# Attention and two MLP layers: float32 P V with columns of ones in the first batch, and MLP activations that read PSUM

## The chip, the cores and the metric

The kernel runs on one core of a Trainium2 chip. The metric is device time in microseconds of one execution, the median of several; lower is better. The engines are TensorE (PE; its weight loads are PEld), VectorE (DVE), ScalarE (ACT), GpSimd (POOL) and SyncE (SP, which issues DMAs).

## The reference, cut to what matters

```python
# q, k, v: (4, 8, 1152, 64) float32; weights float64
q_pool = q.reshape(B, H, S // 2, 2, D).mean(axis=3)           # 576 queries
scores = scale * np.matmul(q_pool, k.transpose(0, 1, 3, 2))
scores = scores - np.max(scores, axis=-1, keepdims=True)
attn = np.exp(scores)
attn = attn / (np.sum(attn, axis=-1, keepdims=True) + 1e-09)
x = np.matmul(attn, v)                    # then to (2304, 512) tokens
h = x @ moe_w_in;  g = np.maximum(0.01 * h, h);                     x = g @ moe_w_out
h = x @ moe2_w_in; g = np.where(h > 0, h, np.exp(np.minimum(h, 0)) - 1); out = g @ moe2_w_out
```

The weights w_in are 512 x 2048 and w_out 2048 x 512.

## The kernel before, in words

Matmuls take float32r operands, which TensorE reads with less precision than float32. Where precision matters an operand is kept as two float32r parts, a rounded one and the residual (`psplit`: a copy, then a subtraction).

**Order.** The kernel records operations with an engine, a cost in ns, a rank and the buffers that it reads and writes (`Program.add`). `Program.schedule` then plays them through as a list scheduler: an engine that falls idle takes the ready operation of lowest rank. Operations are emitted in the order of those start times, so ranks and costs decide what stands where on each engine, and each engine executes its own order strictly. Buffers of one tag are taken in turn; a tile waits for the tile that had its buffer before.

**Attention.** A pair (b, hp) is two heads of a batch; 16 pairs follow each other, 9 ranks apart. For a head, K and the pooled Q are transposed on TensorE (`tr_r`, L391). Row maxima come first: matmuls L466 of 384 keys into tag `s` (two banks), each reduced by VectorE (L470). Then, for each half of the queries (288 columns, `hf`) and each of 9 chunks of 128 keys (`c`), `weigh` makes scores minus the maximum in a bank `e` (L507, L508; in batch 0, `early`, the tags `e` and `h` in turn, four banks), ScalarE takes the exponential twice, once rounded into `pt[:, 0]` (L518) and once in float32 (L520), and VectorE makes the residual `pt[:, 1]` (L522) and adds the float32 values to `pacc` (L526, not for c = 0). `value` multiplies V by both parts (L538) into `o`, a single bank. V lies in `vn` as rounded part and residual side by side in the 128 output rows, so at the end of a half head the lower rows hold the residual's share: ScalarE copies them (L549, `tm`) and VectorE adds them (L551) into `xu`. `pt` has four buffers.

**Scaling.** Once per pair `normalise` sums `pacc` over the keys by float32 matmuls with ones (L568), inverts 10 numbers per partition (L572, L576), spreads and transposes them (L577, L584, L591) and multiplies `xu` (L587, L593).

**MLPs.** `PLAN` starts an MLP per batch and layer every 18 ranks: (0,0), (0,1), (1,0), (1,1) and so on, beside the attention of the following batches. For each of 16 blocks `f` of 128 hidden units and each half, 12 matmuls (L682) fill a bank `h`; there are two, and seven of several tags for batch 3. Layer 0 copies h to SBUF on ScalarE (L693), and VectorE takes max(0.01 t, t) in SBUF (L695). Layer 1 takes exp(h) on ScalarE (L699), min(t, 1) - 1 on VectorE in SBUF (L701) and max(h, t) (L704). The result is split (ScalarE L259, GpSimd L265), and `down` multiplies by w_out (L720) after every four blocks and adds up in SBUF (L733). In the MLPs of batch 0 each weight is first converted from float64 bits (`convert`: VectorE L291, L294, L303, ScalarE, GpSimd) and kept in DRAM for the other batches.

Of the kernel before, what the change touches and what calls it, by code (L numbers as in the profile page):

```python
# [13 lines left out]
ALU = mybir.AluOpType  # L14
# [140 lines left out]
def kernel(  # L155
# [85 lines left out]
    def sb(tag, shape, dt=F32, bufs=1):  # L241
        return prog.buf(tag, bufs, lambda: sp.tile(shape, dt, tag=tag, name=tag, bufs=bufs))
# [4 lines left out]
    def act(n, accum=False, sbuf=False):  # L247
        return 50 + 0.833 * n + (190 if accum else 0) + (43 if sbuf else 0)
# [202 lines left out]
    def prep_v(rank, b, hp, j):  # L451
        vr = raw[b, hp, j, "v"]
        vn = sb("vn", [128, KC, 2 * D], F32R, VB)
        o = D * j
        psplit(rank, KH, "POOL", lambda: vn[:, :, o:o + D], lambda: vn[:, :, D - o:2 * D - o],
               lambda: vr.ap, KC * D, (vn, "h"), [vr], fast=False)
        prep[b, hp, j, "v"] = vn

    def maxima(rank, terms, m, i, early):

# [38 lines left out]
    def weigh(rank, b, hp, j, hf, c, early):  # L499

        cols, parts = half(hf)
        kA, kB, qA, qB = (prep[b, hp, j, n] for n in ("kA", "kB", "qA", "qB"))
        st = pbank("e", F32, (128, 512), early=early)
        ks = slice(128 * c, 128 * c + 128)

        def mm():
            PE.matmul(out=st[:, 0:HB], lhsT=kA[:, ks], rhs=qA[:, cols], start=True, stop=False)  # L507
            PE.matmul(out=st[:, 0:HB], lhsT=kB[:, ks], rhs=qB[:, cols], start=False, stop=True)  # L508

        prog.add("PE", 2 * 133, rank - LS, mm, w=[st],  # L510
                 r=[kA, kB] + [(x, n) for x in (qA, qB) for n in parts])
        pt = sb("pt", [128, 2, HB], F32R, PTB)
        if c == 0 and hf == 0:
            pacc[b, hp, j] = sb("pacc", [128, NQ], F32, 3)
        acc = pacc[b, hp, j]

        p, pw = (lambda: acc[:, cols], (acc, hf)) if c == 0 else (lambda: st[:, 0:HB], st)
        prog.add("ACT", act(HB), rank - LE, lambda: A.activation(  # L518
            out=pt[:, 0], in_=st[:, 0:HB], func=ACTF.Exp), w=[(pt, 0)], r=[st])
        prog.add("ACT", act(HB), rank - LE, lambda: A.activation(  # L520
            out=p(), in_=st[:, 0:HB], func=ACTF.Exp), w=[pw], r=[st])
        prog.add("DVE", dve(HB), rank, lambda: V.tensor_tensor(  # L522
            out=pt[:, 1], in0=p(), in1=f32(pt[:, 0]), op=ALU.subtract), w=[(pt, 1)], r=[pw, (pt, 0)])
        prep[b, hp, j, "pt", hf, c] = pt
        if c:
            prog.add("DVE", dve(HB), rank, lambda: V.tensor_tensor(  # L526
                out=acc[:, cols], in0=p(), in1=acc[:, cols], op=ALU.add), w=[(acc, hf)], r=[pw, (acc, hf)])

    def value(rank, b, hp, j, hf, c, early):
# [4 lines left out]
        o = prep[b, hp, j, "o"]  # L534

        def mm():
            for a in range(2):
                PE.matmul(out=o[:, 0:HB], lhsT=vn[:, c, :], rhs=pt[:, a, :],  # L538
                          start=(c == 0 and a == 0), stop=(c == KC - 1 and a == 1))

        prog.add("PE", 2 * 133, rank, mm, w=[o], r=[vn, pt])
        if c < KC - 1:
            return
        if (b, hp) not in xu:
            xu[b, hp] = sb("xu", [128, NQ], F32, XFB)
        x = xu[b, hp]
        hi, lo = slice(64 * j, 64 * j + 64), slice(64 - 64 * j, 128 - 64 * j)
        tm = sb("tm", [128, HB])
        prog.add("ACT", act(HB), rank - LE, lambda: A.activation(  # L549
            out=tm[hi, :], in_=o[lo, 0:HB], func=ACTF.Copy), w=[tm], r=[o])  # L550
        prog.add("DVE", dve(HB), rank - LE, lambda: V.tensor_tensor(  # L551
# [49 lines left out]
    def attn_pair(at, b, hp):  # L601
# [39 lines left out]
        for u in range(36):  # L641
            j, hf, c = u // 18, u // 9 % 2, u % 9
            event(at + u / 4, weigh, at + u / 4, b, hp, j, hf, c, e)
            event(at + u / 4 + PVLAG, value, at + u / 4 + PVLAG, b, hp, j, hf, c, e)
        event(at + 9 + PVLAG + 0.1, normalise, at + 9 + PVLAG + 0.1, b, hp, e)


    def mlp(at, span, b, layer, xin, w_in, w_out, tags):
# [22 lines left out]
        def up(f):  # L671
# [4 lines left out]
            for hf in range(2):  # L676
# [14 lines left out]
                g32 = t  # L691
                if layer == 0:
                    prog.add("ACT", act(HB), rk, lambda h=h, t=t: A.activation(  # L693
                        out=t.ap, in_=h[:, 0:HB], func=ACTF.Copy), w=[t], r=[h])
                    prog.add("DVE", dve(HB), rk, lambda t=t, g32=g32: V.scalar_tensor_tensor(  # L695
                        out=g32.ap, in0=t.ap, scalar=0.01, in1=t.ap, op0=ALU.mult, op1=ALU.max),
                        w=[g32], r=[t])
                else:
                    prog.add("ACT", act(HB), rk, lambda h=h, t=t: A.activation(  # L699
                        out=t.ap, in_=h[:, 0:HB], func=ACTF.Exp), w=[t], r=[h])  # L700
                    prog.add("DVE", dve(HB, True), rk, lambda t=t: V.tensor_scalar(  # L701
                        out=t.ap, in0=t.ap, scalar1=1.0, scalar2=-1.0, op0=ALU.min, op1=ALU.add),
                        w=[t], r=[t])
                    prog.add("DVE", dve(HB), rk, lambda h=h, t=t, g32=g32: V.tensor_tensor(  # L704
                        out=g32.ap, in0=h[:, 0:HB], in1=t.ap, op=ALU.max), w=[g32], r=[h, t])
                psplit(rk, GH, GL, lambda f=f, cols=cols: g[f][:, 0, cols],
                       lambda f=f, cols=cols: g[f][:, 1, cols], lambda g32=g32: g32.ap, HB,
                       (g[f], hf), [g32], (g[f], 2 + hf))
# [106 lines left out]
```

## Time and profile before

| | |
|---|---|
| median of 3 runs | 1642.79 us (1641.87 to 1644.47) |
| profiled execution, its own time | 1636.31 us |
| its span, first to last instruction | 1634.5 us |
| mean granted TensorE clock | 0.961 of 2.4 GHz |
| busy: PE, PEld, DVE, ACT, POOL | 1485.2, 1380.4, 1271.7, 985.3, 835.5 us |
| instructions: PE, DVE, ACT, POOL | 9984, 2865, 2645, 844 |
| chain that ended last | PE 49%, DVE 32%, ACT 7%, issue 5% |

Busy time is the union of an engine's operations. TensorE's are pipelined, and a matmul's record (300 ns) is longer than the step to the next one, so its busy share says little of how much work it does; counts per stretch of time do. VectorE's records overlap a little as well.

### The profile page before, as it was taken

Reading aid. Unit: us, or ns where it says so; the run is one execution under the profiler, and the core shown is the slowest. Engines: PE = TensorE matmul, PEld = TensorE weight load, DVE = VectorE, ACT = ScalarE, POOL = GpSimd, SP = SyncE. Lnnn points to the kernel's source line nnn. Section 1 sums busy time; section 2 is a strip of 40 time slices with the busy share of each in tenths; the row PEclk is TensorE's granted clock in tenths of the full one; section 3 lists DMA queues with packets and bytes.
Section 4 is the critical chain, followed back from the end, with each engine's and each line's share of the span. In section 5 each row is a group of like instructions: output and inputs, shape, how many; then the busy total and the mean of one; then the engine's idle time right before and its main releaser. Section 6 shows DMA issues by size and latency. Waiting matters only on the chain.

```text
span 1634.5 us, 28876 instructions
## 1 busy us (share of the span) xinstructions
PE 1485.2 (91%) x9984; PEld 1380.4 (84%) x9984; DVE 1271.7 (78%) x2865; ACT 985.3 (60%) x2645; POOL 835.5 (51%) x844
## 2 busy tenths in 40 slices
PE   5898988889888789999999999999999998899898
PEld 3677767778777678899998999899999998898897
DVE  7999999999999999976778778877778666225333
ACT  5675766767567676576665665565666653443432
POOL 6321237656666665455555354545554444456562
PEclk9897988989989999999999999999999999999999
DMA  5221223444344343232222231222222111222221
GB/s 160 89 58 51 78 76 118 143 136 136 116 131 144 125 144 124 59 111 73 83 73 74 57 91 54 87 89 81 81 74 60 46 59 52 87 65 78 71 70 44
DMA packets 85202, 145.00 MB, mean 89 GB/s; under 512 B 9024, under 2 KB 27456, under 8 KB 85056
## 3 DMA queue, kind: packets, MB, share of 16 engines
q1 hardware_dynamic: 85056, 143.17, 29.3%
q8 instruction: 78, 1.28, 0.3%
q14 instruction: 68, 0.56, 0.1%
HBM read 112.20 MB, written 21.50 MB: 82 GB/s over the span
## 4 chain that ended last, share of the span: by engine, by line
PE 49%; DVE 32%; ACT 7%; issue 5%; DMA 3%; POOL 3%; SPq 0%; ACTq 0%; POOLq 0%; DVEq 0%
PE h L720 14%; PE h L682 11%; PE o L538 5%; DVE m L470 5%; DVE pt L522 4%; DVE pacc L526 4%; DVE t L701 3%; PE e L507 3%; DVE wr L303 3%; PE s L466 3%; DVE t L695 3%; PE e L508 2%; DVE ct L294 2%; PE t L568 2%; DVE ct L291 2%
## 5 line engine op out<-in xcount | busy, mean ns | idle before, releaser
L720 PE MATMUL h<-g,wo 128*128 128x288 f32 x2544 | 452.7, 300 | 14.9 <-DVE t L704 8.4
L682 PE MATMUL h<-xs,wi 128*128 128x288 f32 x2520 | 441.7, 310 | 26.9 <-DVE t L704 16.0
L682 PEld LDWEIGHTS h<-xs,wi 128*128 128x128 f32 x2520 | 380.5, 198 | 40.4 <-DVE t L704 22.6
L720 PEld LDWEIGHTS h<-g,wo 128*128 128x128 f32 x2544 | 382.6, 191 | 23.3 <-DVE t L704 7.3
L518 ACT ACTIVATE pt<-e 128x288 fp32r<-128x288 f32 x504 | 203.5, 411 | 204.0 <-PE e L508 193.6
L538 PE MATMUL o<-pt,vn 128*128 128x288 f32 x1152 | 274.2, 317 | 18.2 <-DVE pt L522 16.1
L265 POOL TENSOR_TENSOR wo<-wr,wo 128x512 fp32r<-128x512 f32 x128 | 169.6, 1327 | 229.1 <-ACT wo L259 223.8
L265 POOL TENSOR_TENSOR g<-t,g 128x288 fp32r<-128x288 f32 x256 | 218.7, 862 | 82.7 <-ACT g L259 78.6
L522 DVE TENSOR_TENSOR pt<-e,pt 128x288 fp32r<-128x288 f32 x448 | 201.2, 449 | 49.5 <-ACT e L520 47.6
L538 PEld LDWEIGHTS o<-pt,vn 128*128 128x128 f32 x1152 | 200.6, 199 | 33.0 <-DVE pt L522 28.0
L265 POOL TENSOR_TENSOR wi<-wr,wi 128x512 fp32r<-128x512 f32 x128 | 171.7, 1341 | 75.4 <-ACT wi L259 60.5
L470 DVE TENSOR_REDUCE m<-s 128x1 f32<-128x384 f32 x384 | 201.0, 547 | 5.6 <-PE s L466 5.1
L526 DVE TENSOR_TENSOR pacc<-e,pacc 128x288 f32<-128x288 f32 x448 | 199.7, 446 | 0.3
L520 ACT ACTIVATE e<-e 128x288 f32<-128x288 f32 x448 | 180.7, 409 | 0.3
L507 PE MATMUL e<-qA,kA 128*128 128x288 f32 x504 | 166.4, 331 | 15.2 <-DVE pacc L526 14.4
L466 PE MATMUL s<-kA,qA 128*128 128x384 f32 x384 | 147.9, 405 | 30.1 <-DVE m L470 24.2
L259 ACT ACTIVATE g<-t 128x288 fp32r<-128x288 f32 x256 | 112.3, 445 | 100.2 <-DVE t L704 50.4
L695 DVE SCALAR_TENSOR_TENSOR t<-t 128x288 f32<-128x288 f32 x128 | 101.2, 799 | 79.4 <-ACT t L693 79.1
L508 PE MATMUL e<-qB,kb 65*128 65x288 f32 x504 | 153.3, 305 | 0.0
L301 POOL TENSOR_TENSOR ct<-ct,cr 128x256 uint32<-128x256 uint32 x128 | 101.7, 797 | 99.8 <-DVE ct L294 47.0
L259 ACT ACTIVATE wo<-wr 128x512 fp32r<-128x512 f32 x128 | 80.4, 629 | 110.6 <-PE h L720 46.6
L701 DVE TENSOR_SCALAR t<-t 128x288 f32<-128x288 f32 x128 | 78.4, 613 | 74.5 <-ACT t L699 73.7
(124 smaller groups left out, 2446.9 us busy)
## 6 DMA issues: line engine op xcount, KB each, us to landing
wr<-w SPq DMA_DIRECT2D x192, 256.0 KB, 2.7
cr<-in_moe_w_in_dram SPq DMA_DIRECT2D x64, 256.0 KB, 2.9
cr<-in_moe_w_out_dram SPq DMA_DIRECT2D x64, 256.0 KB, 2.7
w<-wr SPq DMA_DIRECT2D x64, 256.0 KB, 2.4
raw<-in_k_dram SPq DMA_DIRECT2D x32, 288.0 KB, 2.9
raw<-in_v_dram SPq DMA_DIRECT2D x32, 288.0 KB, 2.9
kb<-kA SPq DMA_DIRECT2D x32, 288.0 KB, 3.2
raw<-in_q_dram SPq DMA_DIRECT2D x32, 256.0 KB, 3.0
```

The source lines that it names most:

```text
L259: prog.add("ACT", act(n, sbuf=not psum), rank, lambda: A.activation(out=hi(), in_=src(), func=ACTF.Copy), w=[w], r=r)
L265: lambda: eng.tensor_tensor(out=lo(), in0=src(), in1=f32(hi()), op=ALU.subtract),
L466: PE.matmul(out=st[:, 0:384], lhsT=qa(), rhs=kA[:, 384 * c:384 * c + 384], start=(n == 0), stop=(n == len(terms) - 1))
L470: prog.add("DVE", dve(384), rank, lambda st=st, c=c: V.tensor_reduce(out=m[:, i, c:c + 1], in_=st[:, 0:384], axis=AX.X, op=ALU.max), w=[(m ...
L507: PE.matmul(out=st[:, 0:HB], lhsT=kA[:, ks], rhs=qA[:, cols], start=True, stop=False)
L508: PE.matmul(out=st[:, 0:HB], lhsT=kB[:, ks], rhs=qB[:, cols], start=False, stop=True)
L518: prog.add("ACT", act(HB), rank - LE, lambda: A.activation(out=pt[:, 0], in_=st[:, 0:HB], func=ACTF.Exp), w=[(pt, 0)], r=[st])
L522: prog.add("DVE", dve(HB), rank, lambda: V.tensor_tensor(out=pt[:, 1], in0=p(), in1=f32(pt[:, 0]), op=ALU.subtract), w=[(pt, 1)], r=[pw, ( ...
L526: prog.add("DVE", dve(HB), rank, lambda: V.tensor_tensor(out=acc[:, cols], in0=p(), in1=acc[:, cols], op=ALU.add), w=[(acc, hf)], r=[pw, ( ...
L538: PE.matmul(out=o[:, 0:HB], lhsT=vn[:, c, :], rhs=pt[:, a, :], start=(c == 0 and a == 0), stop=(c == KC - 1 and a == 1))
L682: PE.matmul(out=h[:, 0:HB], lhsT=wi[:, a, c, :], rhs=xs[c][:, e, cols], start=(c == 0 and a == 0 and e == 0), stop=(c == DC - 1 and a == 1))
L720: PE.matmul(out=y[:, 0:HB], lhsT=w[f][1][:, a, d * 128:(d + 1) * 128], rhs=g[f][:, e, cols], start=(f % FC == 0 and a == 0 and e == 0), st ...
```

## The change

In batch 0 (`FULL`): P stays float32 and has one part, one exponential, no residual and no `pacc`. V stays float32; the other 64 columns of `vn` are ones, so that the product holds the sums of P in the other 64 rows. P V is one float32 matmul per chunk. At the end of a half head ScalarE copies the sums plus 1e-9, VectorE inverts them (64 x 288) and multiplies. `normalise` is not called. In all batches the activations change: layer 0 is max(h, 0.01 h) with h from PSUM, layer 1 is Relu(1 - exp(h)) on ScalarE, then max(-t, h) on VectorE.

```diff
+    FULL = (0,)
...
+        if b in FULL:
+            prog.add("POOL", pool(KC * D), rank, lambda: G.tensor_copy(
+                out=f32(vn[:, :, o:o + D]), in_=vr.ap), w=[(vn, "h")], r=[vr])
+            prog.add("POOL", pool(KC * D / 2), rank, lambda: G.memset(
+                f32(vn[:, :, D - o:2 * D - o]), 1.0), w=[(vn, "l")])
+            return
...
+        if b in FULL:
+            prog.add("ACT", act(HB), rank - LE, lambda: A.activation(
+                out=f32(pt[:, 0]), in_=st[:, 0:HB], func=ACTF.Exp), w=[pt], r=[st])
+            return
...
+            if b in FULL:
+                PE.matmul(out=o[:, 0:HB], lhsT=f32(vn[:, c, :]), rhs=f32(pt[:, 0]),
+                          start=(c == 0), stop=(c == KC - 1))
+                return
...
-        prog.add("PE", 2 * 133, rank, mm, w=[o], r=[vn, pt])
+        prog.add("PE", (4 if b in FULL else 2) * 133, rank, mm, w=[o], r=[vn, pt])
...
+        if b in FULL:
+            prog.add("ACT", act(HB), rank - LE, lambda: A.activation(
+                out=tm[hi, :], in_=o[lo, 0:HB], func=ACTF.Copy, bias=1e-9), w=[tm], r=[o])
+            prog.add("DVE", dve(HB), rank - LE, lambda: V.reciprocal(
+                out=tm[hi, :], in_=tm[hi, :]), w=[tm], r=[tm])
+            prog.add("DVE", dve(HB), rank - LE, lambda: V.tensor_tensor(
+                out=x[hi, cols], in0=o[hi, 0:HB], in1=tm[hi, :], op=ALU.mult), w=[(x, (j, hf))], r=[o, tm])
+            return
...
-        event(at + 9 + PVLAG + 0.1, normalise, at + 9 + PVLAG + 0.1, b, hp, e)
+        if b not in FULL:
+            event(at + 9 + PVLAG + 0.1, normalise, at + 9 + PVLAG + 0.1, b, hp, e)
...
-                        out=t.ap, in_=h[:, 0:HB], func=ACTF.Copy), w=[t], r=[h])
-                    prog.add("DVE", dve(HB), rk, lambda t=t, g32=g32: V.scalar_tensor_tensor(
-                        out=g32.ap, in0=t.ap, scalar=0.01, in1=t.ap, op0=ALU.mult, op1=ALU.max),
-                        w=[g32], r=[t])
+                        out=t.ap, in_=h[:, 0:HB], func=ACTF.Copy, scale=0.01), w=[t], r=[h])
+                    prog.add("DVE", dve(HB), rk, lambda h=h, t=t, g32=g32: V.tensor_tensor(
+                        out=g32.ap, in0=h[:, 0:HB], in1=t.ap, op=ALU.max), w=[g32], r=[h, t])
...
-                    prog.add("DVE", dve(HB, True), rk, lambda t=t: V.tensor_scalar(
-                        out=t.ap, in0=t.ap, scalar1=1.0, scalar2=-1.0, op0=ALU.min, op1=ALU.add),
-                        w=[t], r=[t])
-                    prog.add("DVE", dve(HB), rk, lambda h=h, t=t, g32=g32: V.tensor_tensor(
-                        out=g32.ap, in0=h[:, 0:HB], in1=t.ap, op=ALU.max), w=[g32], r=[h, t])
+                    prog.add("ACT", act(HB, sbuf=True), rk, lambda t=t: A.activation(
+                        out=t.ap, in_=t.ap, func=ACTF.Relu, bias=1.0, scale=-1.0), w=[t], r=[t])
+                    prog.add("DVE", dve(HB), rk, lambda h=h, t=t, g32=g32: V.scalar_tensor_tensor(
+                        out=g32.ap, in0=t.ap, scalar=-1.0, in1=h[:, 0:HB], op0=ALU.mult, op1=ALU.max),
+                        w=[g32], r=[h, t])
```

The scheduler makes a new order of all this. Lines of the changed kernel are shifted: L515 and L516 are the score matmuls, L550 the float32 P V, L474 and L478 the maxima and their reductions, L392 the transposes, L568 the reciprocal, L570 the product, L535 and L538 the residual and sum of the other batches, L723, L726 and L728 the three steps of layer 1's activation.

TensorE at the boundary of the third and fourth half head of batch 0, before (`o`, `h`, `e`, `s` are tiles in PSUM; a new number of `o` is a new half head):

```order
L538 MATMUL o_759<-pt_842,vn_238 128x288 x2
L507 MATMUL h_896<-qA_347,kA_277 128x288
L508 MATMUL h_896<-qB_502,kb1_81 128x288
L507 MATMUL h_901<-qA_347,kA_277 128x288
L508 MATMUL h_901<-qB_502,kb1_81 128x288
L466 MATMUL s_910<-kA_751,qA_824 128x384
L466 MATMUL s_918<-kA_751,qA_824 128x384
L466 MATMUL s_924<-kA_751,qA_824 128x384
L466 MATMUL s_927<-kA_751,qA_824 128x384
L538 MATMUL o_930<-pt_857,vn_238 128x288 x2
```

and with the change:

```order
L550 MATMUL o_705<-pt_752,vn_209 128x288
L515 MATMUL h_797<-qA_336,kA_267 128x288
L516 MATMUL h_797<-qB_478,kb1_81 128x288
L515 MATMUL h_804<-qA_336,kA_267 128x288
L516 MATMUL h_804<-qB_478,kb1_81 128x288
L392 MATMUL t_808<-identr_63,qh_577 128x128 x4
L515 MATMUL e_816<-qA_336,kA_267 128x288
L516 MATMUL e_816<-qB_478,kb1_81 128x288
L515 MATMUL e_824<-qA_336,kA_267 128x288
L516 MATMUL e_824<-qB_478,kb1_81 128x288
L515 MATMUL h_830<-qA_336,kA_267 128x288
L516 MATMUL h_830<-qB_478,kb1_81 128x288
```

One transpose and the next half head's first P V follow. Five score pairs and five transposes now stand between the last P V of a half head and the first of the next, where two pairs and four matmuls of maxima stood.

VectorE at the end of the first half head of batch 0, with the change (`m` are maxima; before, this place had one L551 between residuals, sums and reductions):

```order
L568 RECIPROCAL tm_415<-tm_415 64x288
L478 TENSOR_REDUCE m_410<-s_428 128x1
L478 TENSOR_REDUCE m_410<-s_433 128x1
L570 TENSOR_TENSOR xu_442<-o_293,tm_415 64x288
L478 TENSOR_REDUCE m_410<-s_440 128x1
```

At the 16 ends of batch 0 the reciprocal and the product have none to two operations between them, one on average.

VectorE where layer 1 of batch 0 begins, before (`t` is the activation's tile in SBUF, `ct` and `wr` belong to the weight conversion):

```order
L701 TENSOR_SCALAR t_6235<-t_6235 128x288
L294 SCALAR_TENSOR_TENSOR ct<-cr,ct 128x256
L704 TENSOR_TENSOR t_6235<-h,t_6235 128x288
L303 SCALAR_TENSOR_TENSOR wr<-cm,ct 128x256
L526 TENSOR_TENSOR pacc<-e,pacc 128x288
L701 TENSOR_SCALAR t_6266<-t_6266 128x288
```

and with the change:

```order
L728 SCALAR_TENSOR_TENSOR t_5575<-t_5575,h 128x288
L304 SCALAR_TENSOR_TENSOR wr<-cm,ct 128x256
L535 TENSOR_TENSOR pt<-e,pt 128x288
L304 SCALAR_TENSOR_TENSOR wr<-cm,ct 128x256
L538 TENSOR_TENSOR pacc<-e,pacc 128x288
L728 SCALAR_TENSOR_TENSOR t_5605<-t_5605,h 128x288
```

One operation of VectorE per activation is left where two stood.

## Rows read from the trace of the kernel before

**Rows 1.** The page, part 2: busy tenths in 40 slices of 40.9 us.

```profile
PE   5898988889888789999999999999999998899898
...
DVE  7999999999999999976778778877778666225333
```

**Rows 2.** Windows: length; busy us (xcount) of PE, PEld, DVE, ACT, POOL; clock; DMA.

```profile
0.00:28.00 28.00, 11.26 (x35) 6.99 (x36) 18.93 (x37) 11.30 (x22) 19.64 (x30) 1.00 0.50 154
28.00:240.00 212.00, 188.87 (x990) 150.14 (x989) 200.74 (x511) 149.67 (x437) 56.55 (x59) 0.90 0.26 73
240.00:680.00 440.00, 380.23 (x2401) 345.61 (x2402) 426.80 (x959) 294.58 (x808) 278.67 (x293) 0.93 0.41 128
680.00:1385.00 705.00, 677.47 (x4922) 658.24 (x4921) 540.10 (x1198) 437.93 (x1165) 348.93 (x335) 0.99 0.25 73
1385.00:1640.00 255.00, 227.41 (x1641) 219.43 (x1639) 85.11 (x163) 91.83 (x213) 131.73 (x127) 0.99 0.23 68
```

**Rows 3.** Timeline: the first exponential; the last scaling of batch 0.

```profile
28.03 0.41 ACT L518 ACTIVATE pt<-e 128x288 fp32r<-128x288 f32 x1
...
240.02 0.22 DVE L593 TENSOR_TENSOR xu<-t,xu 128x64 f32<-128x64 f32 x1
```

**Rows 4.** Timeline of VectorE near 65 us: start, length, line.

```profile
60.58 1.01 DVE L470 TENSOR_REDUCE m<-s 128x1 f32<-128x384 f32 x2
...
64.90 0.44 DVE L522 TENSOR_TENSOR pt<-e,pt 128x288 fp32r<-128x288 f32 x1
65.26 0.44 DVE L526 TENSOR_TENSOR pacc<-e,pacc 128x288 f32<-128x288 f32 x1
```

**Rows 5.** Windows: 50 us in which TensorE is full.

```profile
800.00:850.00 50.00, 49.74 (x372) 48.90 (x372) 39.08 (x82) 31.54 (x86) 29.61 (x29) 1.00 0.28 83
```

**Rows 6.** Timeline of TensorE: float32 and float32r operations in bursts.

```profile
89.12 2.29 PE L568 MATMUL t<-ones,pacc 128*128 128x2 f32 x20
...
92.99 0.63 PE L584 MATMUL t<-ident,rb 128*128 128x128 f32 x4
...
207.82 0.42 PE L391 MATMUL t<-identr,ql 128*65 128x128 f32 x4 [0.80 <-DVE ql L474]
```

**Rows 7.** Groups by line and shape: xcount, busy us, mean ns, idle before.

```profile
L549 ACT ACTIVATE tm<-o 64x288 f32<-64x288 f32 x64 | 26.0, 406 | 8.6 <-PE o L538 7.1
...
L474 DVE TENSOR_REDUCE ql<-m 128x4 fp32r<-128x12 f32 x32 | 5.0, 155 | 0.0
...
L576 DVE RECIPROCAL r<-r 128x10 f32<-128x10 f32 x16 | 3.4, 210 | 0.2
```

**Rows 8.** Timeline: end of a half head, ScalarE to VectorE.

```profile
234.02 0.40 ACT L549 ACTIVATE tm<-o 64x288 f32<-64x288 f32 x1
...
234.62 0.46 DVE L551 TENSOR_TENSOR xu<-o,tm 64x288 f32<-64x288 f32 x1
```

**Rows 9.** Waits of TensorE, 0 to 250 us: total us, times, longest.

```profile
PE t L391 <- ACT kA L406: 3.2, 8, 0.6
```

**Rows 10.** Groups of VectorE, 240 to 680 us.

```profile
L695 DVE SCALAR_TENSOR_TENSOR t<-t 128x288 f32<-128x288 f32 x32 | 21.6, 677 | 0.4 <-ACT t L693 0.3
...
L701 DVE TENSOR_SCALAR t<-t 128x288 f32<-128x288 f32 x32 | 18.5, 579 | 1.2 <-ACT t L699 1.0
```

**Rows 11.** One line's operations: duration ns min/median/max.

```profile
L701 DVE TENSOR_SCALAR t<-t x128: 290/449/1550, 479.2 to 1615.6; 128x288 f32<-128x288 f32 x128
...
L704 DVE TENSOR_TENSOR t<-h,t x105: 440/448/460, 479.8 to 1609.0; 128x288 f32<-128x288 f32 x105
```

**Rows 12.** Group by line: ScalarE, SBUF to SBUF, 288 wide.

```profile
L259 ACT ACTIVATE g<-t 128x288 fp32r<-128x288 f32 x256 | 112.3, 445 | 100.2 <-DVE t L704 50.4 <-DVE t L695 47.2 <-PE h L720 0.6
```

**Rows 13.** Waits of TensorE, 690 to 860 us (first MLP layer, batch 1).

```profile
PE h L720 <- ACT t L693: 0.3, 1, 0.3
```

**Rows 14.** Waits of TensorE, 877 to 1040 us (second layer, batch 1).

```profile
PE h L682 <- DVE t L704: 5.9, 9, 1.6
PE h L720 <- DVE t L704: 2.9, 1, 2.9
```

More of the change, by code (lines that the diff above doesn't have):

```diff
@@ L454, in prep_v @@
         o = D * j
+        prep[b, hp, j, "v"] = vn
+        if b in FULL:
[4 more added lines that the diff above has]
+            return
         psplit(rank, KH, "POOL", lambda: vn[:, :, o:o + D], lambda: vn[:, :, D - o:2 * D - o],
                lambda: vr.ap, KC * D, (vn, "h"), [vr], fast=False)
-        prep[b, hp, j, "v"] = vn
     def maxima(rank, terms, m, i, early):
@@ L512, in weigh @@
         pt = sb("pt", [128, 2, HB], F32R, PTB)
+        prep[b, hp, j, "pt", hf, c] = pt
+        if b in FULL:
+            prog.add("ACT", act(HB), rank - LE, lambda: A.activation(
+                out=f32(pt[:, 0]), in_=st[:, 0:HB], func=ACTF.Exp), w=[pt], r=[st])
+            return
         if c == 0 and hf == 0:
@@ L523, in weigh @@
             out=pt[:, 1], in0=p(), in1=f32(pt[:, 0]), op=ALU.subtract), w=[(pt, 1)], r=[pw, (pt, 0)])
-        prep[b, hp, j, "pt", hf, c] = pt
         if c:
```

## The prediction

> **What bounds the kernel now.** I read the page's slices first, then the windows by stage, and only then groups and waits inside a stage. The slices [rows 1] show two regimes: VectorE (DVE) is at nine tenths or more up to slice 17, about 700 us, and TensorE (PE) from there to the end. The windows cut this into stages [rows 2]; their borders are the first exponential at 28 us and the last scaling of batch 0 at 240 us [rows 3]. Stage A, 28 to 240 us, is the attention of batch 0 alone: VectorE is busy for 200.7 of 212 us, ScalarE for 149.7, GpSimd for 56.6, and TensorE shows 188.9 us, but with 990 matmuls only. Stage B, 240 to 680 us, holds batch 1's attention, batch 0's two MLPs and the weight conversions: VectorE 426.8 of 440 us. In a full stretch TensorE starts 372 matmuls in 50 us, one each 0.134 us [rows 5], so the 2401 of stage B are about 322 us of work: TensorE waits there. Stage C, 680 us to 1385 us, has 4922 matmuls, 660 us of work in 705: TensorE is the bound. The last stage is the MLPs of batch 3 alone, with TensorE ahead of all others. So work taken from VectorE pays in A and B, one for one at most until TensorE's own work stands in the way, and in C and after only through waits on a PSUM bank.
>
> **Stage A, step by step.** VectorE issues equal operations of 288 elements 0.36 us apart, although one lasts 0.44 us [rows 4]; the step is what it costs. Each of the 16 half heads of batch 0 (4 pairs, 2 heads, 2 halves) has 9 residuals L522 and 8 sums L526. They go: 17 x 0.36 = 6.1 us of the 200.7 / 16 = 12.5 us that VectorE spends on a half head. The scaling chain of a pair goes too. A reciprocal of 288 elements comes.
>
> *The reciprocal.* The trace has only one of 10 elements, 210 ns, beside a reduction of 12 elements in 155 ns [rows 7]. I take 143 ns as fixed (155 less 12 elements at about 1 ns), which leaves 6.7 ns an element: 0.14 + 288 x 6.7 ns = 2.07 us. Low end: the 55 ns above the reduction are paid once, and it costs as the 288-wide sum L551, 0.46 us [rows 8], plus 0.055: 0.51 us. High end: the 0.08 us by which duration exceeds step in rows 4 is no part of its fixed cost, which leaves 0.063, 14.7 ns an element and 4.3 us. I take 2.07, because rows 7 compare two operations of nearly equal size. The Trainium skill, VectorE: DVE Perf Modes, section First, the fixed hardware budget, says that the reciprocal runs on an iterated divide with a repeat count of 8. Eight cycles of its 0.96 GHz would be, as an estimate from that page, 2.5 us, and the sum below would be about 7 us longer; no run here shows that size.
>
> *The float32 matmul.* The program issues 160 matmuls L568, the trace has 320, and 20 take 2.29 us, 0.11 us apart [rows 6]: one float32 matmul is two operations. Four float32 transposes take 0.63 us and four float32r ones 0.42 [rows 6], 0.21 us more for 512 columns, 0.41 ns a column. So I price one of the two at 0.134 + 288 x 0.41 ns = 0.252 us and a chunk of P V at 0.50 us, where two float32r matmuls cost 0.27. Low end: as float32r, 0.27. High end: three further such columns and a weight load (0.11) that nothing hides, 2 x (0.134 + 0.354 + 0.11) = 1.20 us.
>
> *TensorE's own time* for a half head is then 18 score matmuls x 0.134 = 2.4, 9 chunks x 0.50 = 4.5, 7.5 matmuls for the maxima (384 wide, 0.174 by width from 0.134) = 1.3, 9 transposes x 0.06 (from the four in rows 6) = 0.5: 8.8 us, 140 us for 16. VectorE needs 12.5 - 6.1 + 2.0 = 8.4 us less its share of the scaling chain: no longer the bound, but close.
>
> *The single o bank.* The next half's P V waits until the sums are copied, inverted and multiplied. That was copy 0.41 [rows 7] and add 0.46 with a hop of 0.20 between them [rows 8], under a TensorE that waited anyway. Now it is hop 0.2, copy 0.41, hop 0.2, reciprocal 2.07, one reduction 0.47 (none to two stand between in the order above; step from rows 4), product 0.46, hop 0.2: 4.0 us. Against it TensorE has the rows between two o tiles in the order: five score pairs and five transposes in the place shown, 1.6 us, and 2.1 us as a mean over 15 boundaries by the same prices. 1.9 us stay open, 15 times: 28 us. Behind the waiting matmul stands everything of TensorE, since it takes its work in order.
>
> *Sum.* 28 us of start, 140 of work, 28 open, and 3 us that transposes still wait for ScalarE [rows 9]: 199, call it 200 instead of 240. **Stage A gives 40 us.** Off the path, at nothing: 144 second exponentials of ScalarE (it has 62 us to spare [rows 2] and gets 59 more), and V's copy and fill on GpSimd instead of copy and subtraction (busy for 57 of 212 us; without that cover it would be at most 8 x 1.5 us).
>
> **Stage B.** Each of the 32 operations L701 in it goes. They last 579 ns on average [rows 10], less 0.08 of overlap: 32 x 0.50 = 16 us. L695 (677 ns) becomes an operation with h in PSUM. The same kind, L704, lasts 440 to 460 ns, whereas L701, which reads SBUF alone, runs from 290 to 1550 [rows 11]; at 448 it gives 32 x 0.23 = 7.4 us. The second new operation has the form of a product and maximum, which no row shows from PSUM; I take L704's 448, and 677 as the high end, which takes those 7 us back. VectorE falls from 427 to 403 us, still above TensorE's 322, so it stays the bound and **stage B gives 23.5 us**.
>
> **Stage C and the last one.** In layer 1 the bank h was held for exponential, L701 and L704; now Relu on ScalarE stands in the middle, 445 ns by the copy of that size [rows 12] against a median of 449 for L701 [rows 11]: nothing. In layer 0 the bank was free after ScalarE's copy, and TensorE hardly waited, 0.3 us [rows 13]; now it is held over a VectorE operation as well. In the second layer such waits make 8.8 us per MLP [rows 14]. VectorE has a quarter of its time free in C [rows 2], so I take 0 for the sum of both and keep 8.8 a layer for the rival. The last stage has seven banks for it.
>
> **Total.** 1636.3 us of the profiled execution less 40 and 23.5 is 1572.8. The median of the runs shown, 1642.8, is 6.5 us above that execution, and I add them: **1579 us**, 3.9% faster.
>
> **Rivals.** *The reciprocal is cheap* (0.51 us): the open time falls to 0.33 us x 15 = 5, 23 us less, 1556 us. For it: two operations 55 ns apart say little of 288 elements. Against: nothing else in rows 7 explains the 55 ns. *Layer 0 pays for the bank*: 8.8 us in each of the two layer-0 MLPs of stage C, and Relu costs 445 where an undisturbed L701 took 290 [rows 11], 0.155 x 64 in the two second layers: 17.6 + 9.9 = 27.5 more, 1606 us. For it: with two banks TensorE returns to one after 12 matmuls, 1.6 us, which a copy, a maximum and their hops nearly fill. Against: attention matmuls lie between. The Trainium skill, ScalarE: Activation LUTs, section Rules for kernel authors, speaks for this rival: it wants relu and max on VectorE and not on ScalarE. By that rule Relu loses; the trace agrees for the undisturbed operation alone, since with GpSimd beside it VectorE's median is ScalarE's time. *Float32 P V is dear*: at 1.20 us a chunk, 0.70 x 144 = 101 us more on TensorE's path in A, 1680 us, slower by 2.2%. It decides from 0.50 + 64 / 144 = 0.94 us a chunk, where all 64 us are eaten. For it: no row shows a wide float32 matmul; against: the transposes, which stream the same type at 0.41 ns a column more.
>
> **How the numbers follow.** Forecast 0.60, alone good for 1560 to 1596 (the waits of 28 us by half either way, and the 7 us of the product form); cheap reciprocal 0.13; layer 0 pays 0.20; dear float32 0.04; the rest, 0.03, is a new order that helps or hurts in a way I do not see. The range 1540 to 1612 takes in the first three with their own spread, and a reciprocal up to its high end. Measurements of this kernel tell 0.2% from no change. All but the dear float32 case and half of the rest are faster by more: faster 0.94, same 0.02, slower 0.04.
>
> **What would show it.** The reciprocal near 2 us with 288 elements; P V records in pairs 0.25 us apart; batch 0 over by 200 us; TensorE's longest waits in A on o for the product; the two activations' VectorE operations at 0.45 us whatever GpSimd does; MLP layers of batch 0 still at nine tenths of VectorE. If A ends by 180 us, the open time was overrated; if it ends after 230, float32 is dear or the chain is longer; if C, from its first MLP to its last, is more than 10 us longer, layer 0 pays.

## The result, and the profile after

The changed kernel takes 1593.53 us against 1642.33 us: a ratio of 0.9698 with the interval [0.9657, 0.9738], 3.0% faster. In a second session it took 1590.76 us. The forecast was 1579 us, 12 to 15 us too low; both times lie inside its range. The profiled execution of the first session was a disturbed one (3913 us, each MLP matmul 553 ns long instead of 300; with it the median would be 1595.37 us), so the profile after is that of the second session, where the execution took 1588.61 us.

The page of the changed kernel: span, busy time of each engine, busy tenths of TensorE and VectorE in 40 slices of 39.7 us.

```profile
span 1586.8 us, 28364 instructions
...
PE 1457.8 (92%) x9884; PEld 1369.4 (86%) x9884; DVE 1100.4 (69%) x2461; ACT 974.8 (61%) x2621; POOL 812.3 (51%) x852
...
PE   5888889888888889999999999999999999899998
...
DVE  6776579999999999876768676766767564124122
```

VectorE lost 171 us of busy time and the kernel 48 us. In [rows 1] VectorE stood at nine tenths from the second slice on; now it does so only from the seventh to the sixteenth. In the first 230 us neither it nor TensorE is full: batch 0 has lost its bound, and TensorE has not taken its place as the forecast had it.

To put times to it I cut both traces where the first matmul of an MLP starts: (batch 0, layer 0), (1, 0) and (3, 0). Stage A runs from the first exponential to the first of these. The windows of the changed kernel (columns as in [rows 2]), and then those of the kernel before with the same borders:

```profile
28.00:231.00 203.00, 172.03 (x871) 139.47 (x870) 141.57 (x257) 106.91 (x287) 63.76 (x79) 0.92 0.31 87
231.00:681.00 450.00, 396.36 (x2599) 360.64 (x2598) 431.47 (x962) 319.12 (x883) 270.02 (x286) 0.95 0.40 124
681.00:1337.00 656.00, 647.22 (x4712) 636.87 (x4711) 446.00 (x1068) 435.12 (x1184) 327.71 (x324) 0.97 0.26 76
```

```profile
28.00:243.00 215.00, 190.84 (x1003) 151.75 (x1003) 203.74 (x519) 151.82 (x443) 58.02 (x61) 0.90 0.26 74
243.00:705.00 462.00, 402.59 (x2570) 367.32 (x2568) 445.89 (x1006) 308.95 (x846) 283.98 (x297) 0.93 0.40 125
705.00:1379.00 674.00, 649.14 (x4714) 631.14 (x4714) 512.50 (x1136) 420.96 (x1122) 337.58 (x325) 0.99 0.25 74
```

A gave 12 us, B 12, C 18, and the last stage 6 (1379 to 1634.5 before, 1337 to 1586.8 now). The forecast had 40, 23.5, 0 and 0. The sum is near, the places are not. (Each kernel has one trace, and the experiments show that stage A of one and the same order can differ by 7 us between traces.)

The prices were right. One line's operations in the changed kernel (duration ns min/median/max, first and last start):

```profile
L568 DVE RECIPROCAL tm<-tm x16: 1930/1947/1951, 39.3 to 231.5; 64x288 f32<-64x288 f32 x16
...
L570 DVE TENSOR_TENSOR xu<-o,tm x16: 431/455/461, 42.1 to 234.0; 64x288 f32<-64x288 f32 x16
...
L720 DVE TENSOR_TENSOR t<-h,t x105: 435/449/459, 237.5 to 1447.4; 128x288 f32<-128x288 f32 x105
...
L728 DVE SCALAR_TENSOR_TENSOR t<-t,h x105: 432/453/457, 459.4 to 1562.1; 128x288 f32<-128x288 f32 x105
...
L726 ACT ACTIVATE t<-t x128: 426/442/516, 458.4 to 1568.1; 128x288 f32<-128x288 f32 x128
```

The reciprocal lasts 1.95 us (forecast 2.07), the two VectorE operations that read h from PSUM 0.45 us without a tail (0.448), Relu 0.44 (0.445). The float32 P V is here, in TensorE's timeline (start, length, line):

```profile
54.95 0.72 PE L550 MATMUL o<-pt,vn 128*128 128x288 f32 x2
...
55.77 0.65 PE L550 MATMUL o<-pt,vn 128*128 128x288 f32 x2
```

In the second row two records of 406 ns (the line's median) fill 0.65 us, so the second starts 0.24 us after the first: 0.49 us a chunk, forecast 0.50. Among float32r matmuls a chunk can take a little more: the two rows start 0.82 us apart with two score matmuls between them (0.134 us each [rows 5]), which leaves 0.55. But the last product L570 of batch 0 ends at 234.5 us; the forecast had 200.

TensorE's longest waits in stage A with the change (line waited for: total us, times, longest):

```profile
PE s L474 <- DVE m L478: 16.4, 17, 1.9
PE o L550 <- DVE xu L570: 11.9, 7, 2.8
```

The wait for the o bank is there, 7 times and not 15. The larger one is another: the matmuls of the maxima wait for reductions. Two timelines of one moment show why, VectorE first, then TensorE:

```profile
105.10 1.95 DVE L568 RECIPROCAL tm<-tm 64x288 f32<-64x288 f32 x1 [0.71 <-ACT tm L566]
107.08 1.02 DVE L478 TENSOR_REDUCE m<-s 128x1 f32<-128x384 f32 x2
```

```profile
104.86 0.51 PE L474 MATMUL s<-kA,qA 128*128 128x384 f32 x2
...
107.69 0.90 PE L474 MATMUL s<-kA,qA 128*128 128x384 f32 x2 [1.60 <-DVE m L478]
108.60 1.00 PE L550 MATMUL o<-pt,vn 128*128 128x288 f32 x2
```

TensorE has filled both s banks by 105.4 us. VectorE could reduce them, but its queue holds the reciprocal first, and the reciprocal itself waits 0.71 us for ScalarE. The third maxima matmul comes 1.60 us late, and P V stands behind it.

### The profile page after: what moved, and what is told of

The parts are those of the page before. It is cut to its first block, busy times and chain, and to the rows that moved or that the text cites. A ratio compares the mean times of both kernels' runs of the same rounds, so it can differ in the third digit from the quotient of the medians.

```text
span 3911.7 us, 28364 instructions
## 1 busy us (share of the span) xinstructions
PE 3886.4 (99%) x9884; PEld 3450.5 (88%) x9884; DVE 1070.0 (27%) x2461; ACT 1012.1 (26%) x2621; POOL 798.3 (20%) x852
## 4 chain that ended last, share of the span: by engine, by line
PE 99%; DMA 0%; DVE 0%; ACT 0%; issue 0%; SPq 0%; POOL 0%; ACTq 0%; POOLq 0%; DVEq 0%
PE h L745 25%; PE h L707 25%; PE o L554 9%; PE s L474 7%; PE o L550 7%; PE e L515 5%; PE e L516 5%; PE t L392 3%; PE t L592 2%; PE e L745 2%; PE s L707 2%; PE s L745 2%; PE e L707 2%; PE t L707 1%; PE h L515 1%; PE h L516 1%
## 5 line engine op out<-in xcount | busy, mean ns | idle before, releaser
L745 PE MATMUL h<-g,wo 128*128 128x288 f32 x2544 | 1113.1, 630 | 0.0
L707 PE MATMUL h<-xs,wi 128*128 128x288 f32 x2520 | 1081.6, 632 | 0.6 <-DVE acc L758 0.6
L745 PEld LDWEIGHTS h<-g,wo 128*128 128x128 f32 x2544 | 937.4, 395 | 64.2 <-issue 12.4
L707 PEld LDWEIGHTS h<-xs,wi 128*128 128x128 f32 x2520 | 912.3, 390 | 78.8 <-issue 15.4
L554 PE MATMUL o<-pt,vn 128*128 128x288 f32 x864 | 443.1, 645 | 0.0
L515 PE MATMUL e<-qA,kA 128*128 128x288 f32 x504 | 350.1, 695 | 0.0
L478 DVE TENSOR_REDUCE m<-s 128x1 f32<-128x384 f32 x384 | 212.1, 555 | 495.7 <-PE s L474 493.6
L474 PE MATMUL s<-kA,qA 128*128 128x384 f32 x384 | 335.9, 905 | 3.6 <-DVE m L478 2.7
L516 PE MATMUL e<-qB,kb 65*128 65x288 f32 x504 | 331.0, 657 | 0.0
L550 PE MATMUL o<-pt,vn 128*128 128x288 f32 x288 | 302.9, 1203 | 0.0
L535 DVE TENSOR_TENSOR pt<-e,pt 128x288 fp32r<-128x288 f32 x384 | 173.7, 452 | 299.7 <-ACT e L533 298.6
L515 PEld LDWEIGHTS e<-qA,kA 128*128 128x128 f32 x504 | 206.8, 410 | 27.5 <-issue 14.5
L516 PEld LDWEIGHTS e<-qB,kb 65*128 65x128 f32 x504 | 205.4, 408 | 28.0 <-issue 16.2
L474 PEld LDWEIGHTS s<-kA,qA 128*128 128x128 f32 x384 | 154.9, 406 | 50.5 <-DVE m L478 27.1
L538 DVE TENSOR_TENSOR pacc<-e,pacc 128x288 f32<-128x288 f32 x384 | 172.2, 448 | 0.3
L302 POOL TENSOR_TENSOR ct<-ct,cr 128x256 uint32<-128x256 uint32 x128 | 96.5, 755 | 367.3 <-ACT cr L298 131.3
```

Source lines behind the costliest of these rows:

```text
L474: PE.matmul(out=st[:, 0:384], lhsT=qa(), rhs=kA[:, 384 * c:384 * c + 384], start=(n == 0), stop=(n == len(terms) - 1))
L478: prog.add("DVE", dve(384), rank, lambda st=st, c=c: V.tensor_reduce(out=m[:, i, c:c + 1], in_=st[:, 0:384], axis=AX.X, op=ALU.max), w=[(m ...
L535: prog.add("DVE", dve(HB), rank, lambda: V.tensor_tensor(out=pt[:, 1], in0=p(), in1=f32(pt[:, 0]), op=ALU.subtract), w=[(pt, 1)], r=[pw, ( ...
L538: prog.add("DVE", dve(HB), rank, lambda: V.tensor_tensor(out=acc[:, cols], in0=p(), in1=acc[:, cols], op=ALU.add), w=[(acc, hf)], r=[pw, ( ...
L550: PE.matmul(out=o[:, 0:HB], lhsT=f32(vn[:, c, :]), rhs=f32(pt[:, 0]), start=(c == 0), stop=(c == KC - 1))
L707: PE.matmul(out=h[:, 0:HB], lhsT=wi[:, a, c, :], rhs=xs[c][:, e, cols], start=(c == 0 and a == 0 and e == 0), stop=(c == DC - 1 and a == 1))
```

## The experiments

What was open after the result: whether stage C gains through the activations or because batch 0 ends earlier; what eats the gain in stage A, the reciprocal (by the o bank, or by the maxima behind it) or something else; and how much of all this is only the new order. All ratios are against the kernel before, with 95% intervals.

**The change once more, and its two halves.** The first is the changed kernel as it is. The second:

```diff
-    FULL = (0,)
+    FULL = ()
```

The third takes the four activation operations back:

```diff
-                        out=t.ap, in_=h[:, 0:HB], func=ACTF.Copy, scale=0.01), w=[t], r=[h])
-                    prog.add("DVE", dve(HB), rk, lambda h=h, t=t, g32=g32: V.tensor_tensor(
+                        out=t.ap, in_=h[:, 0:HB], func=ACTF.Copy), w=[t], r=[h])
+                    prog.add("DVE", dve(HB), rk, lambda t=t, g32=g32: V.scalar_tensor_tensor(
...
-                    prog.add("ACT", act(HB, sbuf=True), rk, lambda t=t: A.activation(
-                        out=t.ap, in_=t.ap, func=ACTF.Relu, bias=1.0, scale=-1.0), w=[t], r=[t])
+                    prog.add("DVE", dve(HB, True), rk, lambda t=t: V.tensor_scalar(
```

The change again:

> The changed kernel once more, for a trace of an execution like the timed ones. Theory (the o bank): 1587 to 1597 us; the attention of batch 0 ends near 200 us instead of 240, the reciprocal of 64x288 lasts about 2 us, and TensorE waits for the product of the half heads about 15 times by 1 to 2 us. Rival (layer 0 pays for the bank): the attention of batch 0 ends by 200 us or earlier, and the first-layer MLPs of batches 1 and 2 are each some 9 us longer than before.

The activations alone:

> The MLP activations from PSUM in all batches, attention as before. If the parts add up as forecast (24 us from the MLPs, 40 from the attention): 1618 us. If layer 0 pays for the bank: 1635 to 1645 us, no gain. If the MLP part is the larger one: under 1605 us.

The attention alone:

> Float32 P V and columns of ones in batch 0, MLP activations as before. By the forecast of 40 us: 1602 us. If the reciprocal or the float32 matmul eats the gain: 1620 us or more. If layer 0 of the MLPs pays in the full change, this alone is as fast as the whole change or faster, 1585 to 1597 us.

Measured: 1590.76 us, 0.9688 [0.967, 0.9706]; activations alone 1595.45, 0.9721 [0.9703, 0.974]; attention alone 1625.53, 0.9897 [0.9877, 0.9916]. So the activations are worth 46 us and the attention 16, and the two together 51, less than their sum. Stages A, B and C with the activations alone, and stage C with the attention alone:

```profile
28.00:250.00 222.00, 197.15 (x1006) 159.30 (x1005) 205.41 (x521) 153.02 (x444) 58.12 (x62) 0.87 0.25 72
250.00:696.00 446.00, 391.08 (x2568) 353.69 (x2566) 427.60 (x971) 318.04 (x873) 280.05 (x297) 0.97 0.41 130
696.00:1348.00 652.00, 642.57 (x4724) 632.10 (x4722) 449.33 (x1072) 437.15 (x1191) 327.95 (x325) 0.98 0.27 76
```

```profile
694.00:1367.00 673.00, 648.48 (x4715) 630.09 (x4715) 512.96 (x1138) 420.82 (x1123) 337.65 (x325) 0.99 0.26 74
```

Stage C is 652 us with the activations alone and 673 with the attention alone, against 674 before. Its gain belongs to the activations; the rival of an earlier end of batch 0 falls. And stage A is 7 us *longer* (222 against 215) though its attention was not touched. Its order was not touched either: in both traces TensorE, VectorE, ScalarE and GpSimd work on the same tiles in the same sequence up to the first MLP. What differs is the granted clock, 0.87 against 0.90, which is up to 222 x 0.13 - 215 x 0.10 = 7 us. The two kernels of the next experiment also share this order of stage A and take 221 and 218 us for it; the attention alone shares the order of the changed kernel and takes 207 us (28 to 235) for its 203. So differences of up to 7 us in a stage, between one trace and another, are not evidence of a change.

**Layer 0 alone, layer 1 alone.** The activations alone, with one layer's as before (the edit is the matching half of the one above).

> Of the MLP part (46 us faster alone), layer 0's activation alone: max(h, 0.01 h) with h from PSUM; all else as before. If the gain comes from VectorE operations that no longer share SBUF with GpSimd (799 ns before, some 450 now) it gives about half, 1615 to 1622 us. If it comes from layer 1 alone: 1636 to 1645 us. If layer 0 pays for the bank: over 1645 us.

> Of the MLP part, layer 1's activation alone: Relu on ScalarE in place of the scalar operation of VectorE. If the shorter hold of the bank h in layer 1 is the gain (TensorE's waits for the maximum L704 were 20 us in stage C): 1605 to 1615 us. If it is VectorE's time in stage B alone, 16 us by the removed operations: 1624 to 1628 us.

Measured: layer 0 alone 1624.8 us, 0.9909 [0.9883, 0.9936]; layer 1 alone 1610.08, 0.9811 [0.9775, 0.9846]: 17 and 31 us, 48 together against 46 for both. Stage C of each:

```profile
706.00:1371.00 665.00, 646.66 (x4719) 633.48 (x4718) 487.54 (x1140) 419.76 (x1127) 331.46 (x326) 0.98 0.26 75
```

```profile
695.00:1354.00 659.00, 646.33 (x4718) 633.20 (x4717) 472.10 (x1072) 439.51 (x1189) 335.37 (x324) 0.98 0.26 75
```

9 us and 15 us against 674. Layer 0 does not pay for holding its bank. TensorE's longest waits in stage C of the kernel before, and its waits on h for VectorE in that of the changed kernel:

```profile
PE h L682 <- DVE t L704: 9.3, 16, 1.6
PE h L720 <- DVE t L704: 6.2, 3, 3.0
PE s L466 <- DVE m L470: 2.8, 4, 1.4
PE e L507 <- DVE pacc L526: 2.0, 3, 0.9
```

```profile
PE h L745 <- DVE t L728: 3.7, 2, 3.4
PE h L745 <- DVE t L720: 2.3, 5, 0.6
PE h L707 <- DVE t L728: 1.5, 5, 0.4
```

Layer 1's waits fell from 15.5 us to 5.2; layer 0 now waits 2.3 us where the rival asked for 17.6. In stage C of the kernel before, one L701 took 662 ns on average and not its median of 449, and L695 took 881:

```profile
L695 DVE SCALAR_TENSOR_TENSOR t<-t 128x288 f32<-128x288 f32 x64 | 56.4, 881 | 30.0 <-ACT t L693 29.8
L701 DVE TENSOR_SCALAR t<-t 128x288 f32<-128x288 f32 x64 | 42.3, 662 | 30.0 <-ACT t L699 29.4
```

So the step of layer 1 that left VectorE was 0.22 us longer on average than the Relu that replaced it, and besides that it had to take its turn in VectorE's queue. Layer 0's gain comes another way. With layer 0 alone layer 1's waits stay at 14.1 us, but TensorE's waits for VectorE in the attention (the s and e rows above, and 1.5 us more) no longer appear: 6.3 us of the 6.5 by which TensorE's idle time in C falls. VectorE has less to do there, and other banks come free sooner.

**The reciprocal's time taken away.** An ordinary operation of the same size in its place, with the same planned cost, so that the order is the same; batch 0 is then multiplied by a constant and not divided by its sums.

```diff
-            prog.add("DVE", dve(HB), rank - LE, lambda: V.reciprocal(
-                out=tm[hi, :], in_=tm[hi, :]), w=[tm], r=[tm])
+            prog.add("DVE", dve(HB), rank - LE, lambda: V.tensor_scalar(
+                out=tm[hi, :], in0=tm[hi, :], scalar1=0.0, scalar2=0.002, op0=ALU.mult, op1=ALU.add), w=[tm], r=[tm])
```

> The changed kernel with an ordinary scalar operation of the same size, which writes a constant, in place of the 16 reciprocals of batch 0: the division by the sums of batch 0 is left out, the order of all engines is the same. If the reciprocal of about 2 us stands in TensorE's path at the 15 boundaries of half heads, some 20 us faster than the change, about 1570 us. If VectorE's time or other waits cover it: within 5 us of the change.

Measured: 1571.07 us, 0.9553 [0.9519, 0.9587], 20 us less than the change. Stage A and its two waits:

```profile
28.00:213.00 185.00, 167.88 (x869) 136.31 (x868) 120.45 (x256) 106.79 (x287) 64.09 (x79) 0.94 0.33 96
```

```profile
PE s L474 <- DVE m L478: 9.9, 16, 3.6
...
PE o L550 <- DVE xu L570: 2.8, 4, 2.1
```

The stage falls by 18 us, 203 to 185, and both waits with it, from 28.3 to 12.7. The reciprocals are on the path: the operation in their place lasts 0.31 us (median), and 16 of 1.64 us less, 26 us, gave 18. The other waits of the stage, and 6% of its clock, stay when they are gone.

**The bank freed early, and the planner told the price.** The scheduler plans the reciprocal as any operation of 288 elements (0.37 us). One kernel corrects that cost alone:

```diff
-            prog.add("DVE", dve(HB), rank - LE, lambda: V.reciprocal(
+            prog.add("DVE", 1870, rank - LE, lambda: V.reciprocal(
```

The other does so too and has ScalarE copy the product out of o, so that the bank is free after two copies and the product reads SBUF:

```diff
+            un = sb("un", [128, HB])
+            prog.add("ACT", act(HB), rank - LE, lambda: A.activation(
+                out=un[hi, :], in_=o[hi, 0:HB], func=ACTF.Copy), w=[un], r=[o])
...
-                out=x[hi, cols], in0=o[hi, 0:HB], in1=tm[hi, :], op=ALU.mult), w=[(x, (j, hf))], r=[o, tm])
+                out=x[hi, cols], in0=un[hi, :], in1=tm[hi, :], op=ALU.mult), w=[(x, (j, hf))], r=[un, tm])
```

> The changed kernel, where ScalarE also copies the numerators of a half head out of o, so that o is free after two copies (about 1.2 us) and reciprocal and product work in SBUF. The reciprocal's cost in the planner is set to its measured 1.87 us. If the hold of o by the reciprocal is what costs: 1575 us or less, close to the kernel with the plain operation (1571). If the reciprocal costs by its time on VectorE, with reductions queued behind it: 1586 to 1592 us, no gain.

> The changed kernel with the planner's cost of the reciprocal at 1870 instead of 368 ns, nothing else. If the planned order was wrong because of that cost (reductions behind a reciprocal that was thought short): 1578 to 1584 us. If the order matters little: within 4 us of the change, 1587 to 1595 us.

Measured: bank freed early 1557.5 us, 0.949 [0.9447, 0.9532], the best so far; planner cost alone 1568.98, 0.9563 [0.9527, 0.9598]. Stages A and B with the cost alone, and TensorE's waits in A:

```profile
28.00:230.00 202.00, 173.65 (x874) 138.23 (x874) 142.70 (x256) 109.25 (x290) 63.82 (x79) 0.92 0.31 87
230.00:665.00 435.00, 391.00 (x2594) 357.62 (x2594) 419.44 (x962) 319.03 (x880) 271.11 (x286) 0.97 0.42 129
```

```profile
PE s L474 <- DVE m L478: 18.6, 22, 1.8
...
PE o L550 <- DVE xu L570: 0.7, 4, 0.2
```

The same two views with the bank freed early:

```profile
28.00:207.00 179.00, 163.25 (x861) 132.95 (x861) 137.18 (x246) 111.78 (x304) 64.82 (x79) 0.94 0.35 99
207.00:653.00 446.00, 403.61 (x2618) 371.09 (x2617) 425.43 (x976) 320.78 (x888) 271.43 (x286) 0.94 0.41 125
```

```profile
PE s L474 <- DVE m L478: 9.0, 11, 2.5
```

With the cost alone the wait on o all but vanishes (0.7 us) and stage A does not move (202): the planner puts other work before P V, and the maxima (18.6 us for 16.4) and the transposes (6.4 us for 1.6) wait instead. Of the 17 us between the two traces (22 by the medians) 15 lie in stage B, 435 against 450, where only the last reciprocal stands. There the granted clock is 0.97 against 0.95, which is up to 450 x 0.05 - 435 x 0.03 = 9 us; whether the clock is a cause or only a sign of a better order was not separated. With the bank freed as well, A falls by 23 us, to 179, less than the 185 without any reciprocal, and B grows by 11, to 446. So the bank seems to cost what a wait of its own name does not show: whichever instruction stands ahead of P V takes the wait. That is argued from the two runs and not shown by itself, since the copy changes the order as well.

**Three additions to the best kernel.** A third bank for the maxima; the products on GpSimd; batch 1 done as batch 0:

```diff
-    EARLY = {'e': 'eehh'}
+    EARLY = {'e': 'eeh', 's': 'ssh'}
```

```diff
-            prog.add("DVE", dve(HB), rank - LE, lambda: V.tensor_tensor(
+            prog.add("POOL", pool(HB), rank - LE, lambda: G.tensor_tensor(
```

```diff
-    FULL = (0,)
+    FULL = (0, 1)
```

> The kernel with the early copy of o (1557 us), where in batch 0 the maxima take three banks in turn (s, s and h) and the scores three (e, e and h) of the four that they had. If TensorE's waits for the reductions in stage A (12 us there) come from the two banks: 1545 to 1553 us. If they come from reductions that stand behind other work on VectorE: no gain, 1554 to 1565 us.

> The kernel with the early copy of o (1557 us), where GpSimd takes the product of the half heads of batch 0, which has both operands in SBUF there. If VectorE's queue (reductions behind reciprocal and product) still binds stage A: 1546 to 1554 us, 16 operations of 0.36 us less on VectorE and no reduction behind a product. If TensorE's own work and clock bind A by now: within 4 us of 1557.

> The kernel with the early copy of o (1557 us), with float32 P V in batches 0 and 1. Theory (stage B is bound by VectorE at 0.36 us an operation): 272 residuals and sums less and 16 reciprocals of 1.87 us more take 68 us off VectorE in B, TensorE gains 33 us of work; 1500 to 1530 us. Rival (TensorE's order and waits bind there as in stage A, where half of the gain was lost): 1530 to 1550 us. Slower than 1557: the single o bank with only two e banks binds.

Measured: third bank 1562.4 us, 0.952 [0.9494, 0.9546]; GpSimd 1558.67, 0.948 [0.9449, 0.9511]; batch 1 too 1565.76, 0.9539 [0.952, 0.9558]. None gains; the last is 8 us slower by the medians, with intervals of the ratios that overlap. With the third bank the maxima's wait in A falls from 9.0 to 5.3 us, and TensorE waits for exponentials instead, 3.7 us, now that scores have three banks and not four. The last is the instructive miss; its stage B:

```profile
209.00:659.00 450.00, 395.61 (x2514) 356.70 (x2513) 367.45 (x702) 280.78 (x757) 273.90 (x293) 0.98 0.40 125
```

VectorE is busy for 58 us less than in the best kernel (367 against 425), and the stage is 4 us longer. So VectorE's time is not what bounds stage B here. TensorE waits on h for the two activations and the accumulation, 35 us in all in this trace, and has 32 us more of float32 work (144 chunks, 0.22 us each above two float32r matmuls).

**The planner told the conversions' prices.** If a true cost helped for the reciprocal, it might for the conversions, which the planner has too cheap. In the best kernel:

```diff
-            prog.add("DVE", dve(CW, True), rank, lambda r=r, t=t: V.tensor_scalar(
+            prog.add("DVE", 400, rank, lambda r=r, t=t: V.tensor_scalar(
...
-            prog.add("DVE", dve(CW), rank, lambda r=r, t=t: V.scalar_tensor_tensor(
+            prog.add("DVE", 500, rank, lambda r=r, t=t: V.scalar_tensor_tensor(
...
-            prog.add("DVE", dve(CW), rank, lambda n=n, t=t, mag=mag: V.scalar_tensor_tensor(
+            prog.add("DVE", 600, rank, lambda n=n, t=t, mag=mag: V.scalar_tensor_tensor(
```

> The kernel with the early copy of o (1557 us), where the planner's costs of the three conversion operations on VectorE are set near what they take in stage B (400, 500 and 600 instead of 199, 335 and 335 ns). If the gain of the reciprocal's true cost was the order that a true cost makes: 1535 to 1550 us, as 324 such operations are planned too short in B. If it was particular to the reciprocal, or chance in how the order falls: 1550 to 1570 us.

Measured: 1575.48 us, 0.9592 [0.9568, 0.9615], 18 us slower than the best kernel, although stage A became shorter still (173 us). Stage B took 470:

```profile
201.00:671.00 470.00, 413.67 (x2617) 379.09 (x2615) 424.13 (x976) 322.31 (x887) 271.78 (x286) 0.91 0.38 119
```

The gain of the reciprocal's true cost in stage B is thus a matter of that particular order, not proof that true costs make better plans. The conversions' own time looks like the reason, and is not. VectorE's two first conversion steps in stage B, the change and then the change with the reciprocal's cost:

```profile
L295 DVE SCALAR_TENSOR_TENSOR ct<-cr,ct 128x256 uint32<-128x256 uint32 x106 | 66.7, 632 | 0.4
...
L292 DVE TENSOR_SCALAR ct<-cr 128x256 uint32<-128x256 uint32 x106 | 57.9, 549 | 3.5 <-DMA cr<-in_moe_w_in_dram 1.9 <-DMA cr<-in_moe_w_out_dram 1.5
```

```profile
L295 DVE SCALAR_TENSOR_TENSOR ct<-cr,ct 128x256 uint32<-128x256 uint32 x106 | 61.2, 579 | 0.4
L292 DVE TENSOR_SCALAR ct<-cr 128x256 uint32<-128x256 uint32 x106 | 48.7, 462 | 2.6 <-DMA cr<-in_moe_w_in_dram 1.5 <-DMA cr<-in_moe_w_out_dram 0.9
```

The same 212 operations take 14.7 us less, and the stage is 15 us shorter. But in the run just told they take 109.2 us, as little as the 109.9 of the second pair, in a stage of 470 us. What goes along with the stage's length in these runs is the granted clock: 0.97 in 435 us, 0.95 in 450, 0.91 in 470, and for the last against the best kernel (0.94 in 446) that is up to 16 of 24 us. It is not the whole of it: with batch 1 too the stage took 450 us at 0.98. Why one order is better than another stays open.

## Why the prediction was right in its number

The direction, the size within about 1% and nearly every price held. The stages did not, and that the sum came near is luck: two errors of opposite sign cancelled in part. A and B were overrated by 40 us, C and the last stage underrated by 24.

- *Prices.* Reciprocal 1.95 us for 2.07; chunk of P V 0.49 to 0.55 for 0.50; the two activation steps 0.449 and 0.453 for 0.448. The rivals of a cheap reciprocal and of a dear float32 fall by these rows. The Trainium skill, VectorE: DVE Perf Modes, section First, the fixed hardware budget, gives the iterated divide a repeat count of 8, from which the forecast had 2.5 us as that page's estimate. The trace does not agree with that estimate: from 210 ns for 10 elements [rows 7] to 1947 ns for 288 is 6.25 ns an element, so the way from two small operations of the trace came closer.
- *Stage A, the step "Sum".* This step failed. It added 28 us for o and 3 us for transposes to TensorE's work at full speed, and ended at 200 us; batch 0 ends at 234.5. The forecast's reading of an end after 230, a dear float32 or a longer chain, does not hold either: the rows of both are near their prices. The total idle time was right by chance: 203 us less 172 busy is the same 31. But of it 12 are on o and 16 on the maxima, whose reductions queue on VectorE behind the reciprocal and other work (9.9 us stay without the reciprocals); the forecast did not have them. What it left out is in the busy part: 172 us for 140 us of work. The granted clock of the stage, 0.92 against 0.90 before [rows 2], takes up to 203 x 0.08 = 16 us. Of the other 16 the longer chunks of P V are at most 144 x 0.06 = 9 us, an estimate from the 0.55 above; the rest, probably short stops that a record longer than its step covers, was not separated. The clock stood in the rows of before and was priced at nothing. The reciprocals themselves cost 18 us here, shown by the run without them in the same order; what freeing the bank gave in the better plan, 23 us in A and 11 in the whole, is of the bank and the new order together.
- *Stage B, one for one.* 12 us for 23.5. VectorE did stay near full, 431 of 450 us, and the stage shrank about as its busy time did (14 us). But VectorE's busy time fell by less than the two removed steps, because the conversion steps L292 and L295 took 549 and 632 ns where the kernel before, in its stage B, had 473 and 573. And the run with batch 1 too shows where the rule ends: VectorE had 58 us less to do there and the stage was no shorter.
- *Stage C, the term "nothing".* It failed: 18 us for 0, and 6 in the last stage. The forecast set Relu's 445 ns against L701's median; the mean of that stage was 662, and the long tail to 1550 stood in its own rows [rows 11]. Layer 1's waits on its bank are 10 of the 18 us; most of the rest of TensorE's idle time that went is the attention's, as layer 0 alone shows.
- *Layer 0 pays.* Refuted: 2.3 us of waits, and layer 0 alone gains 17 us. The Trainium skill, ScalarE: Activation LUTs, section Rules for kernel authors, wants relu and max on VectorE, for its speed with bf16. In this kernel, whose operands are float32, the trace disagrees: with Relu on ScalarE layer 1 alone gained 31 us. ScalarE had room (busy for 421 of the 674 us of stage C), and L701 on VectorE took 0.29 to 1.55 us [rows 11].

## What to carry to other kernels

In a program whose engines take their work strictly in order, price a new long operation by what queues behind it on its own engine, not only by the bank that it holds: of the waits of stage A more were on the maxima than on the bank, and when the planner removed the second the first grew. Compare a moved step by the mean of its stage, tail and turn in the queue included, never by the median. And where a list scheduler makes the order, some 20 us of a result can be the new order alone (one planned cost gained 22 us, three others lost 18), so an edit is judged by a run in which the planned costs are the same (as with the reciprocal replaced) or by the stage in which it lies, and a stage by more than a difference of 7 us.

## What the runs showed of the hardware

A stop of TensorE can be followed by a lower granted clock. Windows of the changed kernel around the wait shown above (columns as in [rows 2]): before it, the wait itself, and what follows.

```profile
104.30:106.20 1.90, 1.60 (x10) 1.05 (x8) 1.19 (x2) 1.85 (x6) 1.90 (x2) 1.00 0.74 227
106.20:107.60 1.40, 0.00 (x0) 0.00 (x0) 1.37 (x3) 0.26 (x1) 0.16 (x1) 1.00 0.36 94
107.60:109.20 1.60, 1.48 (x5) 0.90 (x5) 1.60 (x5) 0.00 (x0) 0.00 (x0) 0.91 1.03 343
109.20:112.00 2.80, 2.80 (x8) 2.09 (x8) 1.83 (x5) 1.46 (x4) 0.73 (x1) 0.50 0.40 151
```

TensorE stood still for 1.6 us at a granted clock of 1.00. By 1.5 us after it had begun again the clock was at 0.50, the lower of its two levels (1.2 of 2.4 GHz), and stayed there for at least 2.8 us, which cost up to 1.4 us more. That the stop caused the fall is not shown, and not every stop has one behind it. In this window TensorE stands still for 2.6 us, up to 96.5 us, and the clock stays at 1.00:

```profile
93.80:100.50 6.70, 4.06 (x24) 3.09 (x24) 5.85 (x11) 3.47 (x11) 3.99 (x5) 1.00 0.34 107
```

A granted clock of 0.92 is a sixth of stage A at the lower level. It rose to 0.94 where the reciprocals' time or the bank's was taken away. But in the kernel before, where TensorE idles for 24 of the 215 us and not for 31 of 203, it was 0.90.
